# A gated mix of linear attention and SwiGLU: the third piece of wq and wk on ScalarE's DMA queue

## The chip, the cores and the metric

The kernel runs on one core of one Trainium2 chip. The metric is the device time of one execution, in microseconds (us), lower being better. A core has TensorE (PE, with weight loads listed apart as PEld), VectorE (DVE), ScalarE (ACT), GpSimd (POOL) and SyncE (SP). Every engine has an instruction stream of its own, and the streams meet only at semaphores. DMAs are issued by an engine's stream and carried out by 16 DMA engines that the queues share. In this kernel nearly all DMAs are issued by SP (queue q1 in the profile), and one by ACT (q10).

## The reference

One input x (2048 tokens of 512 values, bf16) goes through two blocks, and a gate mixes what they give. Multiplications are in bf16 and sums in fp32.

```python
def A(x, wqkv, wo):                     # 32 heads of 16
    q, k, v = split(x @ wqkv)
    phi = lambda t: where(t > 0, t + 1, exp(t)) + 1e-6
    pq, pk = phi(q), phi(k)
    kv, z = einsum("bhsd,bhse->bhde", pk, v), pk.sum(over tokens)
    o = (pq @ kv) / (pq . z + 1e-6)
    return o @ wo

def B(x, w1, w3, w2):                   # hidden size 1376
    return (silu(x @ w1) * (x @ w3)) @ w2

g = sigmoid((x * gate_w).sum(-1, keepdims=True))
out = g * A(x, wqkv, wo) + (1 - g) * B(x, w1, w3, w2)
```

## The kernel before, in words

**Stages.** The tokens are cut into 16 tiles of 128. In the first stage (0 to about 46 us of the span) each tile is projected onto k and q (`project`, the matmuls of line 183; the four contraction chunks of 128 are called `kc`), `phi` makes pk and pq of them with one ACT activation and two DVE instructions, and `g_step` (line 231) sums x-transposed times pk over all tokens into four PSUM banks. From these sums v's part follows later, so v itself is never computed. The second stage runs four blocks of 512 tokens: the SwiGLU matmuls (lines 303 and 309), and then the output matmuls of both blocks and the mix (lines 475, 492 and 498). Stores leave on SP's queue.

**The order.** The schedule is written by hand: the program's order of instructions on each engine is the order in which they run, and nothing is reordered. The waits between engines follow from what each instruction reads and writes, region by region of a tile.

**The start.** wq and wk lie side by side in one tile, `wqk`, of four contraction chunks; a "piece" is one chunk, 128 partitions by 1024 bf16 values (256 KB), loaded by one call of `load_wqk` (line 126). SP issues, in this order: x's first 256 tokens in natural layout (line 129), the four pieces, and then for each further tile a load of x that transposes it on the way (`load_xT`, line 123), with natural copies of x in between (line 141), and the weights of the later stages (lines 143 to 156). ACT's stream begins with an activation of one column, `act_pre` (line 130), whose result nobody reads and before which ACT loads its table. The next instruction of its stream is the issue of a small DMA of its own, `touch` (line 133), which reads the first 16 columns of pieces two to four into a tile that nobody reads. ACT's next work after that is line 380, a copy of a transposed part of x out of PSUM.

**PE at the start.** PE runs 13 matmuls on a constant (line 359), transposes the first 256 tokens of x by matmuls with an identity matrix (line 365), and then runs the k and q matmuls of the first two tiles interleaved by piece: four on the first piece, two transposes for the fourth chunk of x, four on the second piece, then k's two on the third and two on the fourth, and q's four on the third and fourth. The k projection of tile 2 follows, the first to use an x that SP's transposing loads brought.

```python
    for kc in range(2):
        for n, t in (("k", 0), ("q", 0), ("k", 1), ("q", 1)):
            first_mm(n, t, kc)
        if kc == 0:
            transpose_kc(3, bank[0])
            nc.vector.tensor_copy(out=xT[:, 3, 0 : 2 * P], in_=bank[0][:, 0 : 2 * P])
    for kc in range(2, KC):
        for t in range(2):
            first_mm("k", t, kc)
```

Of the kernel before, what the change touches and what calls it, by code (L numbers as in the profile page):

```python
# [8 lines left out]
ACT = mybir.ActivationFunctionType  # L9
# [3 lines left out]
BF16 = mybir.dt.bfloat16  # L13
# [3 lines left out]
def kernel(  # L17
# [17 lines left out]
    nc = tc.nc  # L35
    P = nc.NUM_PARTITIONS

    Bb, S, D = A_x.shape
# [23 lines left out]
    wqkv_r = A_wqkv.rearrange("(kc d) n -> d kc n", d=P)  # L62
# [3 lines left out]
    consts = ctx.enter_context(tc.tile_pool(name="consts", bufs=1))  # L66
# [5 lines left out]
    warm = nc.const_aps.tensor(1.0, [P, 256], BF16)  # L72
# [7 lines left out]
        out=bmask[:], in_=bmask[:], pattern=[[-Dh, HPC], [0, Dh]], compare_op=ALU.is_ge,  # L80
# [3 lines left out]
        out=bmask[:], in_=bmask[:], pattern=[[Dh, HPC], [0, Dh]], compare_op=ALU.is_ge,  # L84
# [23 lines left out]
    wqk = consts.tile([P, KC, 2 * D], BF16, name="wqk")  # L108
# [6 lines left out]
    w3 = consts.tile([P, KC, F0], BF16, name="w3")  # L115
    w2 = consts.tile([P, FC, D], BF16, name="w2")
    xT = consts.tile([P, KC, S], BF16, name="xT")
    act_pre = consts.tile([P, 1], BF16, name="act_pre")
    dq = nc.sync

    def load_xT(t):
        ts = slice(t * P, (t + 1) * P)
        dq.dma_start(out=xT[:, :, ts], in_=x2d[ts, :], transpose=True)

    def load_wqk(kc):
        dq.dma_start(out=wqk[:, kc, :], in_=wqkv_r[:, kc, 0 : 2 * D])

    x_first = x2d[0 : 2 * P, :].rearrange("(p j) d -> p j d", j=2)
    dq.dma_start(out=xN[:, 0:2, :], in_=x_first)  # L129
    nc.scalar.activation(out=act_pre[:], in_=warm[:, 0:1], func=ACT.Exp)  # L130

    touch = consts.tile([P, KC - 1, 16], BF16, name="touch")
    nc.scalar.dma_start(out=touch[:], in_=wqkv_r[:, 1:KC, 0:16])
    for kc in range(KC):
        load_wqk(kc)
    natural = {3: (2, 4), 5: (4, 8), 8: (8, 16)}
    for t in range(2, NT):
        load_xT(t)
# [3 lines left out]
    with nc.allow_non_contiguous_dma(reason="gate column"):  # L142
        dq.dma_start(
            out=wr[:, :, 2 * FR : NR], in_=gate_w.rearrange("(kc d o) -> d kc o", d=P, o=1)
# [3 lines left out]
    for w, w_r, cuts in ((w1, w1_r, (0, KC)), (w3, w3_r, (0, KC))):  # L148
# [8 lines left out]
        out=w2x[:].rearrange("p r d -> p (r d)"),  # L157
        in_=w2x_r[None].to_broadcast([TPB, RP, RG * D]),
# [442 lines left out]
```

## Time and profile before

| what | value |
|---|---|
| median of 3 runs | 178.73 us (178.44 to 178.74) |
| the profiled execution's own time | 177.74 us |
| its span, first to last instruction | 176.0 us |
| PE busy | 171.3 us, 97% |
| DVE, POOL, ACT busy | 110.5, 63.3, 59.1 us |
| first k matmul of PE | 4.41 us into the span |
| end of the first stage | about 46 us |

The profile is of one execution. Its times count from the first instruction of the span. A line of the timeline gives start, duration, engine, source line (L126 is line 126), operation, the tiles written and read, and in square brackets how long the engine had sat idle and what ended that; a "q" behind an engine's name (SPq, ACTq) marks an instruction of its sequencer, here a DMA issue. PE's matmuls are pipelined, so that the duration of one overlaps the next. The chain is the chain of work that ended last, followed back from the end. "Landing" is the time from the start of a DMA's issue to its completion semaphore.

### The profile page before, as it was taken

The numbers are of one execution on the slowest core, as the hardware profiler recorded it, in microseconds if no ns is written. First come the engines' busy times: TensorE is split into PE (matmuls) and PEld (weight loads), VectorE is DVE, ScalarE is ACT, GpSimd is POOL, SyncE is SP. The second block draws the span as 40 slices with busy tenths as digits, with TensorE's granted clock in tenths as the row PEclk, the third lists the DMA queues.
The fourth block names the chain that finished last, engine by engine and source line by source line (L and its number), as shares of the span: only waits on it lengthen the run. The fifth ranks groups of instructions, "written<-read, shape, count | busy, mean of one in ns | idle before, by whom it ended". The sixth has DMA issues, their size and how long they took to land.

```text
span 176.0 us, 2668 instructions
## 1 busy us (share of the span) xinstructions
PE 171.3 (97%) x952; PEld 82.4 (47%) x969; DVE 110.5 (63%) x207; ACT 59.1 (34%) x109; POOL 63.3 (36%) x106
## 2 busy tenths in 40 slices
PE   8999999999999999999999999999999999999993
PEld 5444444444456443444444466444444444444453
DVE  0399788888764899777343477853435775344363
ACT  4364544544753533322433101224226122422000
POOL 5087656656300668586300044540000662000000
DMA  5988969997205112323200013330000233000001
GB/s 172 277 197 207 164 123 237 403 352 231 78 4 56 22 30 41 78 63 91 58 0 0 0 34 84 84 89 0 0 4 0 60 89 89 4 0 0 30 30 60
DMA packets 29360, 15.58 MB, mean 88 GB/s; under 512 B 21156, under 2 KB 27556, under 8 KB 29348
## 3 DMA queue, kind: packets, MB, share of 16 engines
q1 hardware_dynamic: 28948, 15.41, 35.1%
q8 instruction: 7, 0.11, 0.3%
q10 hardware_dynamic: 400, 0.01, 0.1%
q14 instruction: 5, 0.04, 0.1%
HBM read 8.86 MB, written 2.10 MB: 62 GB/s over the span
## 4 chain that ended last, share of the span: by engine, by line
PE 95%; DMA 2%; issue 1%; SPq 0%; DVE 0%
PE bank L303 20%; PE bank L492 20%; PE bank L309 19%; PE bank L183 16%; PE bank L231 8%; PE bank L475 8%; PE bank L245 3%; DMA wqk<-in_A_wqkv_dram 2%; PE bank L278 2%; PE bank L447 0%; SPq L129 0%; PE bank L462 0%; DVE o L498 0%; PE bank L365 0%
## 5 line engine op out<-in xcount | busy, mean ns | idle before, releaser
L315 DVE TENSOR_TENSOR hT<-bank,sg 128x512 bf16<-128x512 f32 x40 | 27.3, 682 | 31.0 <-PE bank L309 28.9
L303 PE MATMUL bank<-xT,w 128*128 128x512 bf16 x158 | 40.8, 379 | 0.2
L309 PE MATMUL bank<-xT,w 128*128 128x512 bf16 x156 | 40.5, 379 | 0.2
L314 ACT ACTIVATE sg<-bank 128x512 bf16<-128x512 f32 x40 | 23.9, 597 | 45.9 <-PE bank L303 45.9
L492 PE MATMUL bank<-w,hT 128*128 128x512 bf16 (+2 forms) x176 | 37.0, 355 | 0.5 <-issue 0.3
L337 POOL TENSOR_TENSOR pqs<-pq,rden 128x512 bf16<-128x512 bf16 x16 | 16.9, 1057 | 54.3 <-issue 46.8
L183 PE MATMUL bank<-wqk,xT 128*128 128x512 bf16 x126 | 30.2, 379 | 0.1
L215 POOL TENSOR_TENSOR zacc<-zacc,pk 128x128 f32<-128x128 f32 x56 | 23.3, 447 | 10.4 <-DVE pk L201 10.4
L492 PEld LDWEIGHTS <-hT 128*128 128x128 bf16 x180 | 16.7, 98 | 18.4 <-issue 0.8
L309 PEld LDWEIGHTS <-w 128*128 128x128 bf16 x160 | 15.7, 98 | 18.9
L303 PEld LDWEIGHTS <-w 128*128 128x128 bf16 x160 | 15.5, 98 | 18.2 <-issue 0.2
L498 DVE SCALAR_TENSOR_TENSOR o<-bank,omg_all,aga 128x512 bf16<-128x512 f32 (+2 forms) x18 | 12.4, 692 | 14.5 <-PE bank L492 11.7
L183 PEld LDWEIGHTS <-xT 128*128 128x128 bf16 x128 | 12.5, 98 | 14.9 <-issue 0.3
L322 POOL TENSOR_TENSOR pr<-pq,zb 128x512 f32<-128x512 bf16 x16 | 18.4, 1155 | 0.1
L231 PE MATMUL bank<-pk,xN 128*128 128x512 bf16 x62 | 16.3, 379 | 0.2
L475 PE MATMUL bank<-M,pqT 128*128 128x512 bf16 x61 | 15.6, 379 | 0.1
L196 ACT ACTIVATE eq<-bank 128x512 bf16<-128x512 f32 x16 | 9.4, 597 | 16.0 <-PE bank L183 14.9
L201 DVE SCALAR_TENSOR_TENSOR pk<-bank,emk 128x512 bf16<-128x512 f32 x16 | 11.1, 692 | 1.6
L196 ACT ACTIVATE ek<-bank 128x512 bf16<-128x512 f32 x16 | 9.4, 597 | 6.5 <-PE bank L183 6.5
L201 DVE SCALAR_TENSOR_TENSOR pq<-bank,emq 128x512 bf16<-128x512 f32 x16 | 11.1, 692 | 0.5
L326 DVE TENSOR_REDUCE den<-pr 128x32 f32<-128x512 f32 x16 | 10.8, 676 | 0.0
L231 PEld LDWEIGHTS <-xN 128*128 128x128 bf16 x64 | 6.3, 98 | 7.5
(54 smaller groups left out, 95.6 us busy)
## 6 DMA issues: line engine op xcount, KB each, us to landing
w<-in_B_w_dram SPq DMA_DIRECT2D x3, 1280.0 KB, 10.3
out_dram<-o SPq DMA_DIRECT2D x15, 128.0 KB, 1.9
wqk<-in_A_wqkv_dram SPq DMA_DIRECT2D x4, 256.0 KB, 3.7
xN<-in_A_x_dram SPq DMA_DIRECT2D x1, 1024.0 KB
xN<-in_A_x_dram SPq DMA_DIRECT2D x2, 256.0 KB, 2.9
xN<-in_A_x_dram SPq DMA_DIRECT2D x1, 512.0 KB, 4.2
wv<-in_A_wqkv_dram SPq DMA_DIRECT2D x1, 512.0 KB, 11.2
wo<-in_A_wo_dram SPq DMA_DIRECT2D x1, 512.0 KB, 12.2
```

Source lines behind the costliest of these rows:

```text
L183: nc.tensor.matmul(ps[:], lhsT=xT[:, kc, t * P : (t + 1) * P], rhs=w[:, kc, :], start=(kc == 0), stop=(kc == KC - 1),)
L196: nc.scalar.activation(out=e[:], in_=ps[:], func=ACT.Exp)
L201: nc.vector.scalar_tensor_tensor(out=dst, in0=ps[:], scalar=0.0, in1=em[:], op0=ALU.max, op1=ALU.add)
L215: nc.gpsimd.tensor_tensor(out=(zaccb if t == NT - 1 else zacc)[:, cs], in0=zacc[:, cs], in1=pk[t][:, cs], op=ALU.add,)
L231: nc.tensor.matmul(bank[kc][:], lhsT=xN[:, t, kc * P : (kc + 1) * P], rhs=pk[t][:], start=(t == 0), stop=(t == NT - 1),)
L303: nc.tensor.matmul(g_ps[:], lhsT=w1[:, kc, fs], rhs=xT[:, kc, tok], start=(kc == 0), stop=(kc == KC - 1),)
L309: nc.tensor.matmul(u_ps[:], lhsT=w3[:, kc, fs], rhs=xT[:, kc, tok], start=(kc == 0), stop=(kc == KC - 1),)
L314: nc.scalar.activation(out=sg[:], in_=g_ps[:], func=ACT.Silu)
L315: nc.vector.tensor_tensor(out=hT[tb][:, fc, :], in0=u_ps[:], in1=sg[:], op=ALU.mult)
L322: nc.gpsimd.tensor_tensor(out=pr[t][:], in0=pq[:, t, :], in1=zb[:], op=ALU.mult)
L475: nc.tensor.matmul(ps[:], lhsT=pqT[:, c, ts], rhs=M2[:, c, :], start=(c == 0), stop=(c == KC - 1),)
L492: nc.tensor.matmul(ps[:, 0 : cs.stop - cs.start], lhsT=hT[tb][:, fc, tt * P : (tt + 1) * P], rhs=w2[:, fc, cs], start=(fc == 0 and not sta ...
```

## The change

The third piece (`kc` of 2) is issued on ACT's queue, and the other three stay on SP's in their order. ACT's first activation no longer writes a tile of its own but the first column of the third piece in `wqk`. The DMA that loads the third piece writes the same column, so it waits until that activation has finished. In ACT's stream it comes after `touch`. The tile `act_pre` goes.

```diff
@@ -115,24 +115,23 @@
-    act_pre = consts.tile([P, 1], BF16, name="act_pre")
     dq = nc.sync
...
-    def load_wqk(kc):
-        dq.dma_start(out=wqk[:, kc, :], in_=wqkv_r[:, kc, 0 : 2 * D])
+    def load_wqk(kc, queue):
+        queue.dma_start(out=wqk[:, kc, :], in_=wqkv_r[:, kc, 0 : 2 * D])
 
     x_first = x2d[0 : 2 * P, :].rearrange("(p j) d -> p j d", j=2)
     dq.dma_start(out=xN[:, 0:2, :], in_=x_first)
-    nc.scalar.activation(out=act_pre[:], in_=warm[:, 0:1], func=ACT.Exp)
+    nc.scalar.activation(out=wqk[:, 2, 0:1], in_=warm[:, 0:1], func=ACT.Exp)
 
     touch = consts.tile([P, KC - 1, 16], BF16, name="touch")
     nc.scalar.dma_start(out=touch[:], in_=wqkv_r[:, 1:KC, 0:16])
     for kc in range(KC):
-        load_wqk(kc)
+        load_wqk(kc, nc.scalar if kc in (2,) else dq)
```

## The prediction, made before the result was known

> **What bounds the kernel now.** I read the page's busy time and its chain first, then the chain from 3 to 10 us, then the start in order of time, then the transfers.
>
> ```profile
> PE 171.3 (97%) x952; PEld 82.4 (47%) x969; DVE 110.5 (63%) x207; ACT 59.1 (34%) x109; POOL 63.3 (36%) x106
> ...
> PE 95%; DMA 2%; issue 1%; SPq 0%; DVE 0%
> ```
>
> TensorE is busy for 97% of the span and makes 95% of the chain, so what shifts its stream near the start shifts the end by as much. The list of waits has none of PE on a DMA after 7 us that could take a shift back; its few idle spots later are waits on ACT and DVE, which follow PE, and lost records. The only DMA in the chain (2%) is one the change touches:
>
> ```profile
> 1.26 3.11 DMA wqk<-in_A_wqkv_dram
> 4.37 0.04 issue
> 4.41 1.02 PE bank L183 x4
> 5.43 0.11 PE bank L365 x2
> 5.54 3.60 PE bank L183 x16
> ```
>
> From 4.41 PE runs four matmuls on the first piece, two transposes, four on the second, two each on the third and fourth. A matmul of 512 columns follows the last after 0.216 us. The second piece's start at 5.38, the third's at 6.25, and the fourth's would at 6.68 but do at 6.83, after a weight load that sat idle:
>
> ```profile
> 6.83 0.96 PEld L183 LDWEIGHTS <-xT 128*128 128x128 bf16 x5 [0.27 <-issue]
> ```
>
> So the fourth piece costs PE 0.15 us and the others nothing. The issues at the start, SP's queue and ACT's:
>
> ```profile
> 0.81 0.39 SPq L129 DMA_DIRECT2D xN<-in_A_x_dram  x1
> 1.26 1.84 SPq L126 DMA_DIRECT2D wqk<-in_A_wqkv_dram  x4
> 3.15 1.30 SPq L123 DMA_TRANSPOSE xT<-in_A_x_dram  x1
> ```
>
> ```profile
> 0.80 1.28 ACT L130 ACT_TABLE_LOAD   x1 [0.80 <-PEq L585]
> 0.86 0.43 ACTq L133 DMA_DIRECT2D touch<-in_A_wqkv_dram  x1
> 2.10 0.20 ACT L130 ACTIVATE act_pre<-const-bfloat16-1.0 128x1 bf16<-128x1 bf16 x1
> ```
>
> The four pieces are issued at 1.26, 1.72, 2.20 and 2.67, 0.47 apart. The DMA view of a window with one issue in it gives each one's time to landing: 3.1, 3.4, 3.9 and 4.1 us. With the trace's own ends that is 4.37, 5.17, 6.06 and 6.78 (x landed at 3.60). They land 0.72 to 0.89 apart, so it is the transfer that paces them, not the issue. A piece is there 0.21 us (second) and 0.19 us (third) before use; that is all the slack.
>
> The queues between 2.9 and 3.2 us, q10 being ACT's and q1 SP's, with packets, MB and share of 16 engines:
>
> ```profile
> q10 hardware_dynamic: 359, 0.01, 67.3%
> q1 hardware_dynamic: 43, 0.06, 50.2%
> ```
>
> ACT's small DMA takes the engines when x is through, ahead of SP's first piece, and nearly alone: where both have work, one goes as a run and the other stands.
>
> **The change part by part.** *Removed:* a 128x1 tile; the activation stays, with the same size and its table load, and ends at 2.30. *SP's queue:* one issue fewer, so the fourth piece is issued at 2.20 and the transposed loads, natural x and weights behind it all 0.47 us sooner. PE waits for none of them: the first transposed load landed at 7.28 for a use at 8.12. Worth 0. If they were late instead, that 0.84 is the cover.
>
> *ACT's queue:* one issue of 0.43 us more. It waits for the activation: 2.30 plus 0.05 (from the releaser's end to an issue or matmul in these rows) is 2.35, so it ends near 2.79. Behind it stands ACT's copy of the transposed x (L380), which starts at 4.08 and waits 1.78 us for PE. 1.3 us of that is left over, so the cost is 0; without that cover it would be 0.43 on the way to the first q and k matmuls.
>
> *Where the third piece falls among the transfers* is the term that counts. From the end of its issue x took 0.72 us to its first packet (1.20 to 1.92, idle engines). ACT's touch took 1.6 us or more (1.29 to between 2.90 and 3.05), but x held the engines for that time. So the third piece stands at the engines between 2.79 + 0.72 = 3.5 and 2.79 + 1.6 = 4.4. I take 3.5, since the longer one has its reason in x. x's last bytes ran near 3.0 and it landed at 3.60; by that lag of some 0.5 us the first piece's bytes end near 3.85 and the second's near 4.65. At 3.5 the first piece is still running and the second stands queued.
>
> If ACT's queue gets its turn there, as touch did after x, the order of landings is first, third, second, fourth in the same four places, since the bytes are the same. The second then lands at 6.06 instead of 5.17. PE starts it at 6.06 + 0.04 = 6.10 instead of 5.38: +0.72. Four matmuls later, at 6.96, the third is long there; at 7.40 the fourth (6.78) is too, so the 0.15 us wait goes. Sum +0.72 - 0.15 = +0.57 us. Were the two queues to share packet by packet, the first would land later but the second still third, and the sum is the same.
>
> The Trainium skill has two rules on this, in "DMA: Bandwidth & Descriptors". "Issuing engines are not separate DMA queues" says that transfers from SP and ACT run on the same 16 engines, and a second issuer saves only issue time. The landings 0.72 to 0.89 us apart on issues 0.47 apart agree; by it the gain is 0 of the 0.47. "Queues, rings and completion order" says that each engine goes round the queues and empties a whole packet of descriptors before it switches. By that rule the third piece follows the first and the sum is +0.57; by order of age (the touch row, issued before the first piece, fits that as well) it is the +0.43 below.
>
> Ends: below, -0.15 (only the fourth piece's wait goes; PE cannot begin before 4.37, when its transposes end, so the first piece has 0.04 more at most). Above, +0.72 with 0.2 more for a switch of queues, the time that touch held the engines, less 0.15: about +0.8.
>
> **The sum** is against the profiled execution: 177.74 + 0.57 = 178.31, its span 176.0 + 0.57 = 176.6 and 1.74 around it. That execution lies 0.99 below the median of the three runs, so on the median: 178.73 + 0.57 = 179.30.
>
> **The rivals.**
> *Order of age.* The third piece's issue ends at 2.79, after the fourth's (2.20 to 2.63), and it goes last. It lands at 6.78, and PE, which takes it before the fourth, starts it at 6.83 instead of 6.25: +0.58 - 0.15 = +0.43, 179.16. For it: touch ran in order of age too. Against: it needs one line for both queues, and the page shows two.
>
> *Order kept.* If ACT's transfers do take 1.6 us from issue to engine, the third piece arrives at 4.4, during the second, and runs where it ran. Then 0 to -0.15: 178.6 to 178.73, no change. For it: the touch row is the only one on ACT's queue. A higher place of the same kind: should PE be on its slow clock longer in other executions (256 columns took 0.213 us before 3.6 us, 512 take 0.216 after 4.4), it would reach the second piece later and hide the late landing.
>
> *Faster.* Two queues leave fewer gaps at the engines: a 2 KB packet takes 84 ns, so a piece's 8 packets per engine need 0.67 us against 0.72 to 0.89. The fourth would land at 3.60 + 4 x 0.67 = 6.28 and nothing waits. In the profiled execution that is worth 0.15 + 0.04 at most, 0.1%. It decides only if the 0.99 us by which the shown runs lie above the profiled one is the same wait, and at least 0.17 us of it goes too; with half of it, 178.73 - 0.15 - 0.5 = 178.1. No row shows what those runs wait for.
>
> *The clock.* PE would stand still from 5.43 to 6.10. Should that bring back the slow rate for as long as it held at first (0.84 to about 4.1), it costs half of 3.3 us: 178.73 + 0.57 + 1.65 = 180.95. No row shows a stop of that length near the start.
>
> **How the numbers follow.** Third piece ahead of the second, +0.57: 0.42. Order of age, +0.43: 0.14. Order kept: 0.32. Faster: 0.07. Clock: 0.05. The forecast is the first, 179.3 us. A measurement of this kernel tells about 0.2% (0.36 us) from no change. So slower holds 0.42 + 0.14 + 0.05 = 0.61, less 0.03 for a second piece that lands some 0.2 us sooner than I take: 0.58. Within 0.2%: 0.35. Faster: 0.07. The range takes in the kept order with the 0.15 gain and a spread of 0.2 below (178.4), and reaches above the forecast by 0.3, to the upper end of +0.8 and a little spread (179.6). It leaves out the clock and most of faster, some 0.15 with the noise. The forecast's own range is 179.1 to 179.6.
>
> **What would show it.** ACT's issue of the third piece at 2.35, SP's transposes from 2.67. Landings: second near 6.06, third near 5.17, fourth near 6.8. A PE wait for the second piece of 0.6 to 0.7 us ending near 6.1 and none at the fourth; PE's first matmul at 4.41 as before. Wrong if the second still lands by 5.4: then the order was kept. A wait before the third piece to about 6.8 is the order of age.

## The result and the profile after

The change makes the kernel slower: the median goes from 178.39 us to 179.12 us over 22 runs each, a ratio of 1.0045 with a 95% interval of 1.0034 to 1.0056. That is 0.6 to 1.0 us. The forecast was +0.57.

The page of the changed kernel's profiled execution (178.61 us, span 176.8), busy times and chain:

```profile
PE 173.1 (98%) x969; PEld 82.5 (47%) x969; DVE 110.9 (63%) x207; ACT 59.1 (33%) x109; POOL 63.2 (36%) x106
...
PE 96%; DMA 2%; DVE 0%; issue 0%
```

TensorE is still the bound, and no other engine has over 0.4 us more work (the 1.8 us more of PE go with 17 matmul records more than in the profile before, and with a slower start, below). The issues at the start, ACT's and SP's (line numbers are one lower than before):

```profile
0.87 0.44 ACTq L132 DMA_DIRECT2D touch<-in_A_wqkv_dram  x1
2.10 0.20 ACT L129 ACTIVATE wqk<-const-bfloat16-1.0 128x1 bf16<-128x1 bf16 x1
2.33 0.36 ACTq L125 DMA_DIRECT2D wqk<-in_A_wqkv_dram  x1
```

```profile
0.81 0.39 SPq L128 DMA_DIRECT2D xN<-in_A_x_dram  x1
1.25 1.37 SPq L125 DMA_DIRECT2D wqk<-in_A_wqkv_dram  x3
2.67 1.30 SPq L122 DMA_TRANSPOSE xT<-in_A_x_dram  x1
```

The change did what it says: the third piece is issued at 2.33, 0.03 us after the activation, and SP's transposed loads start 0.47 us sooner. What landed when, by the trace's own ends, is the core of the matter. "First G" is PE's first matmul on pk (L231 before), and "rest" the span from there to its end:

| profile | first | second | third | fourth | first G | rest |
|---|---|---|---|---|---|---|
| before | 4.37 | 5.17 | 6.06 | 6.78 | 8.98 | 167.06 |
| changed, 1st | 4.53 | 5.19 | 7.08 | 6.68 | 9.71 | 167.07 |
| changed, 2nd (after_again) | 4.46 | 5.13 | 6.99 | 6.81 | 9.61 | 167.06 |
| changed, 3rd (after_third) | 4.35 | 6.58 | 7.63 | 7.50 | 10.26 | 167.06 |

The rest of the kernel is 167.06 to 167.15 us in all 14 profiles of this study, whatever came ahead. So all that the change costs within the span is lost before the first G, as the forecast had it, and nothing is given back.

A smaller part lies outside the span. Every run has its time and its span on record (spans to 0.1 us). The time is longer than the span by 1.85 us on the mean in the changed kernel (1.80 to 1.92 in single runs), and by 1.71 in the kernel before (1.65 to 1.78). So 0.14 of the 0.73 us is spent where no view looks; on what, is not shown.

Where it is lost depends on the execution. The chain of the first profile of the changed kernel, from 3 us on:

```profile
0.81 2.99 DMA xN<-in_A_x_dram
3.79 0.05 issue
3.84 0.82 PE bank L364 x6
4.66 1.54 PE bank L182 x4
6.21 0.11 PE bank L364 x2
6.32 3.55 PE bank L182 x16
```

There is no piece in it. x landed 0.19 us later than in the profile before, and the four matmuls on the first piece took 1.54 us, not 1.02: PE's slow clock lasted to about 6 us. PE came to the third piece at 7.02 and waited 0.10 us for it. So this pair of profiles, 0.73 us apart at the first G, shows hardly any of what the change costs; that the difference fits is chance. (The kernel before without touch, with all pieces on SP's queue and the slow clock too, has its first G at 9.70.) The third profile, whose time (179.17 us) is nearest to the median, shows the cost:

```profile
1.72 4.86 DMA wqk<-in_A_wqkv_dram
6.58 0.04 issue
6.62 1.02 PE bank L182 x4
7.64 0.03 issue
7.67 2.75 PE bank L182 x12
```

PE waits for the second piece until 6.62, and after it for the third, whose first matmul starts at 7.67. The row of PE's wait in the timeline:

```profile
6.62 1.64 PE L182 MATMUL bank<-wqk,xT 128*128 128x512 bf16 x6 [0.83 <-DMA wqk<-in_A_wqkv_dram]
```

How the transfers ran is seen in a window from 4.8 to 5.6 us. Before:

```profile
DMA packets 159, 0.30 MB, mean 371 GB/s; under 512 B 14, under 2 KB 14, under 8 KB 159
## 3 DMA queue, kind: packets, MB, share of 16 engines
q1 hardware_dynamic: 159, 0.30, 96.7%
```

and in the first profile of the changed kernel:

```profile
DMA packets 136, 0.28 MB, mean 348 GB/s; under 512 B 0, under 2 KB 0, under 8 KB 136
## 3 DMA queue, kind: packets, MB, share of 16 engines
q10 hardware_dynamic: 67, 0.14, 50.5%
q1 hardware_dynamic: 69, 0.14, 46.9%
```

A piece is 128 packets of 2 KB, and ends on each engine with one packet of 4 bytes. Before, 14 such ends fall into these 0.8 us. After, the two queues move nearly the same number of packets and no engine ends any piece. So in this profile third and fourth run in turn and end together. They land 0.40, 0.18 and 0.12 us apart in the three profiles, against 0.72 before. The second profile is less clean. There the fourth ended on 12 of the 16 engines within the same window, and had landed on 15 by 6.18; it landed at 6.81 because of one engine. The third, too, had its last packet on one engine half a microsecond after those on the others (6.54 against 6.06).

### The profile page after: what moved, and what is told of

It is laid out like the page before. It is cut to its first block, busy times and chain, and to the rows that moved or that the text cites. A ratio compares the mean times of both kernels' runs of the same rounds, so it can differ in the third digit from the quotient of the medians.

```text
span 176.8 us, 2685 instructions
## 1 busy us (share of the span) xinstructions
PE 173.1 (98%) x969; PEld 82.5 (47%) x969; DVE 110.9 (63%) x207; ACT 59.1 (33%) x109; POOL 63.2 (36%) x106
## 4 chain that ended last, share of the span: by engine, by line
PE 96%; DMA 2%; DVE 0%; issue 0%
PE bank L491 20%; PE bank L302 20%; PE bank L308 20%; PE bank L182 16%; PE bank L230 8%; PE bank L474 8%; PE bank L244 3%; DMA xN<-in_A_x_dram 2%; PE bank L277 2%; PE bank L364 1%; PE bank L446 0%; PE bank L461 0%; DVE o L497 0%
## 5 line engine op out<-in xcount | busy, mean ns | idle before, releaser
L302 PE MATMUL bank<-xT,w 128*128 128x512 bf16 x160 | 41.1, 379 | 0.0
L308 PE MATMUL bank<-xT,w 128*128 128x512 bf16 x160 | 41.1, 379 | 0.0
L491 PE MATMUL bank<-w,hT 128*128 128x512 bf16 (+2 forms) x180 | 37.5, 355 | 0.0
L182 PE MATMUL bank<-wqk,xT 128*128 128x512 bf16 x128 | 31.0, 384 | 0.0
L474 PE MATMUL bank<-M,pqT 128*128 128x512 bf16 x64 | 16.1, 379 | 0.0
```

Of the source, the lines that this page charges most:

```text
L182: nc.tensor.matmul(ps[:], lhsT=xT[:, kc, t * P : (t + 1) * P], rhs=w[:, kc, :], start=(kc == 0), stop=(kc == KC - 1),)
L302: nc.tensor.matmul(g_ps[:], lhsT=w1[:, kc, fs], rhs=xT[:, kc, tok], start=(kc == 0), stop=(kc == KC - 1),)
L308: nc.tensor.matmul(u_ps[:], lhsT=w3[:, kc, fs], rhs=xT[:, kc, tok], start=(kc == 0), stop=(kc == KC - 1),)
L474: nc.tensor.matmul(ps[:], lhsT=pqT[:, c, ts], rhs=M2[:, c, :], start=(c == 0), stop=(c == KC - 1),)
L491: nc.tensor.matmul(ps[:, 0 : cs.stop - cs.start], lhsT=hT[tb][:, fc, tt * P : (tt + 1) * P], rhs=w2[:, fc, cs], start=(fc == 0 and not sta ...
```

## The experiments

Each run shares its comparison with runs of the kernel before on the same chip. The times to landing and first packets are from each run's one profile.

**A second profile, the hold alone, PE's order turned, the fourth piece moved.** The first theories were that the third piece is late (L), that PE's clock is what differs (C), and that the hold costs the time (H).

*after_again* is the changed kernel unaltered.

> The changed kernel once more, for a second profile of it. Theory L (late piece): the third piece stands at the engines only some 1.8 us after its issue ends, shares them packet by packet with the fourth, and lands last, at 6.9 to 7.2 us; PE waits for it, so the ratio is 1.003 to 1.006, and in an execution whose PE is on its fast clock by 4.4 us the wait ahead of the third piece's first matmul is 0.6 to 0.9 us. Theory C (clock): the changed kernel is slower since PE's fast clock comes later in it (5.9 us in the profile after against about 4.1 before); then matmuls 0.43 us apart on the first piece are seen here too, and the third piece's landing costs 0.1 us or nothing.

1.0046 (1.0031 to 1.0062). The third landed at 6.99, last. PE's clock was slow to about 5.7 us here too, and the wait at the third piece only 0.11. As far as this profile goes, C was not ruled out.

*hold_on_sp* has the activation write into the third piece, and all four pieces on SP's queue:

```diff
-        load_wqk(kc, nc.scalar if kc in (2,) else dq)
+        load_wqk(kc, dq)
```

> The hold alone: the activation writes into the third piece, all four pieces stay on SP's queue. SP's third issue moves from 2.20 to 2.35 us and all behind it by 0.15. Theory L: the transfer paces the pieces, so the third still lands near 6.06 and the fourth near 6.8; ratio 0.999 to 1.001. Theory H (the hold is what costs): the third piece lands later by the hold and PE waits; ratio 1.003 to 1.005.

1.0005 (0.9987 to 1.0024). The pieces landed at 4.32, 4.97, 5.63 and 6.40, in order. The hold, 0.13 us on SP's queue, costs nothing that could be measured.

*after_pe_swap* lets PE take the fourth piece ahead of the third:

```diff
...
-    for kc in range(2, KC):
+    for kc in (3, 2):
         for t in range(2):
             first_mm("k", t, kc)
...
-    for kc in range(2, KC):
+    for kc in (3, 2):
         first_mm("q", 0, kc)
-    for kc in range(2, KC):
+    for kc in (3, 2):
         first_mm("q", 1, kc)
```

The accumulations of these matmuls end on the third piece instead of the fourth.

> The changed kernel, but PE takes the fourth piece ahead of the third for the first two tiles; no DMA differs from the changed kernel. Theory L: the fourth (landed 6.68) is used from about 6.7, the third (7.08) from about 7.15, four or so matmuls of 0.216 us lie between what is there and what is late, and most of the loss goes: ratio 1.000 to 1.002. Theory C or one in which SP's earlier transposed loads cost the time: ratio stays 1.0035 to 1.0055.

1.0042 (1.0021 to 1.0062): nothing came back, and L in that form fell. The ratio is the one that C gave. In this profile, however, the fast clock was there by 5.1 us: the second piece landed at 6.50 and PE waited for it, and the fourth (7.48) was as late as the third (7.66).

*fourth_on_act* moves the fourth piece instead of the third (the hold with it):

```diff
-    nc.scalar.activation(out=wqk[:, 2, 0:1], in_=warm[:, 0:1], func=ACT.Exp)
+    nc.scalar.activation(out=wqk[:, 3, 0:1], in_=warm[:, 0:1], func=ACT.Exp)
...
-        load_wqk(kc, nc.scalar if kc in (2,) else dq)
+        load_wqk(kc, nc.scalar if kc in (3,) else dq)
```

> The fourth piece instead of the third on ACT's queue, held by the activation writing into it; the third on SP's. Theory L: the fourth comes to the engines near 4.5 us, shares them with the third, and lands last near 7.1, the third near 6.7; PE starts the third at about 6.72 instead of 6.25 and the fourth at 7.12 instead of 6.83: +0.3 us, ratio 1.001 to 1.003. A theory by which ACT's queue takes its turn right after the first piece: the fourth lands second, third and second piece a place later, ratio 1.003 to 1.004.

1.0040 (1.0027 to 1.0053), more than expected. The second landed at 5.05, so ACT's queue did not take its turn after the first piece. The third, although it stayed on SP's queue, landed at 7.13, the fourth at 7.50. PE's clock was fast by 4.4 us, and the wait stands alone in PE's timeline:

```profile
5.41 1.03 PE L182 MATMUL bank<-wqk,xT 128*128 128x512 bf16 x4
7.17 0.59 PE L182 MATMUL bank<-wqk,xT 128*128 128x512 bf16 x2 [0.74 <-DMA wqk<-in_A_wqkv_dram]
```

Here the loss is there with a fast clock, so C does not explain it. Sharing may not be all of it either. The third had landed on 13 of the 16 engines by 6.14, and three reads of 2 KB took 0.70, 0.85 and 1.23 us (between 4.15 and 4.28, ahead of ACT's first packet), against the usual 84 ns. From this came theory S: a piece on ACT's queue makes the piece beside it late as well, whichever of the two is moved; both end when the last byte is there.

**What the joint landing costs without ACT's queue.** *pair_on_sp* is the kernel before with third and fourth loaded by one DMA on SP's queue:

```diff
-    for kc in range(KC):
+    for kc in range(2):
         load_wqk(kc)
+    dq.dma_start(out=wqk[:, 2:4, :], in_=wqkv_r[:, 2:4, 0 : 2 * D])
```

> The kernel before, with the third and the fourth piece loaded by one DMA of 512 KB on SP's queue, so that both are there only when the last byte is; ACT's queue carries no piece. Theory S (sharing): what the change costs is first of all that the third piece, moved packet by packet beside the fourth, lands with it at the end of all four instead of a place ahead. Then this kernel shows that part alone: both land near 6.8, PE starts the third at about 6.83 instead of 6.25 and does not wait for the fourth, +0.43 us, ratio 1.001 to 1.0035. If the late landing of both costs nothing by itself: 0.999 to 1.001.

1.0034 (1.0019 to 1.0048), 0.6 us. Both landed at 6.62, earlier than the fourth did before, and PE waited for them in front of the third:

```profile
5.76 0.86 PE bank L184 x4
6.63 0.03 issue
6.66 2.75 PE bank L184 x12
```

```profile
6.66 1.39 PEld L184 LDWEIGHTS <-xT 128*128 128x128 bf16 x7 [0.31 <-issue]
```

This is the experiment that carries the explanation. It has no second queue, no hold and, in its profile, no later last byte (SP's transposed loads start 0.47 us sooner here too, on which see the next run). What it takes away is the third piece's place ahead of the fourth. Its time outside the span is that of the kernel before (1.71). Within the span its runs are 0.56 us longer on the mean than those of the kernel before, and those of the changed kernel 0.56 and 0.68 (in *after_third* and *after_again*). The interval is wide, 0.34 to 0.86 us, and the expected 0.43 lies in it. Its profile shows less: PE waited 0.19 us (a matmul was due at 6.47), and the first G came 0.27 later than before. But that execution, 178.10 us, was the fastest of 12, and no profile shows where a middling one loses its time.

**When ACT's transfer comes to the engines.** In the four profiles so far with a held piece on ACT's queue, its first 2 KB packet ran at 4.58 to 4.68 us, 1.9 to 2.0 after the issue's end. *xt_late* holds SP's first transposed load:

```diff
+    nc.gpsimd.memset(xT[:, 0, 2 * P : 2 * P + 1], 0.0)
     x_first = x2d[0 : 2 * P, :].rearrange("(p j) d -> p j d", j=2)
```

> The changed kernel, with SP's first transposed load held by a write of GpSimd into one column of its destination, so that it is issued near 3.5 us instead of 2.67; the third piece is issued as in the changed kernel (2.33 to 2.69). In four profiles with a piece on ACT's queue its first 2 KB packet ran at 4.58 to 4.68 us, 0.61 to 0.71 after the end of SP's first transposed load's issue (3.95 to 3.97), the lag that x has after its own (0.64 to 0.73). Theory D (one writer of descriptors for both queues, and ACT's request waits behind SP's transposed load): the first packet comes at 3.3 to 3.6. Theory Q (ACT's queue takes some 1.9 us from the end of an issue whatever SP does): it stays at 4.5 to 4.7. Time: by D the third piece shares with the first and second, second lands late, ratio 1.001 to 1.005; by Q the transposed load no longer runs beside it, ratio 1.002 to 1.004.

The transposed load was issued at 3.39, and the first packet of the third piece still came late, at 4.82. So theory D fell. The ratio was 1.0043 (1.0023 to 1.0062), just over what Q gave; third and fourth landed at 7.15 and 6.97. SP's transposed loads start later here than in the kernel before (3.39 against 3.15), so their earlier start isn't the cause in the changed kernel either.

*no_hold* gives the activation its own tile again and leaves the third piece on ACT's queue:

```diff
-    nc.scalar.activation(out=wqk[:, 2, 0:1], in_=warm[:, 0:1], func=ACT.Exp)
+    nc.scalar.activation(out=act_pre[:], in_=warm[:, 0:1], func=ACT.Exp)
```

> The third piece on ACT's queue, not held: the activation writes a tile of its own, the issue follows touch at about 1.31 to 1.75 us. Theory Q: its first packet at 3.5 to 3.7, so it shares the engines with the first and second pieces, which land 0.3 to 0.8 us late; ratio 1.002 to 1.006. Theory D: its descriptors are written between two of SP's pieces, first packet at 2.9 to 3.3, the first piece lands near 5 us; ratio 1.003 to 1.008. Theory H (the hold is what costs): ratio 0.998 to 1.001.

First packet at 3.61, 1.76 after the issue's end: as Q had it. 1.0026 (1.0008 to 1.0044). But the third did not share with the second, as Q had expected. ACT's queue ran alone between the first and the second piece, as this window from 4.0 to 4.25 us shows, in which SP's queue has no packet:

```profile
q10 hardware_dynamic: 46, 0.09, 94.7%
```

The third had landed on 15 of the 16 engines by 5.07, and the second, behind it, by 5.75. One engine brought them only at 6.44 and 6.64 (one read on ACT's queue took 1.01 us, at 3.85), and the fourth landed at 7.18. So this run has the order that was forecast for the changed kernel, and each piece went as a run. It is slower than the kernel before all the same, though 0.14 of the 0.46 us lies outside the span (1.85 against 1.71).

*after_no_touch* and *before_no_touch* leave touch out of the changed kernel and of the kernel before:

```diff
-    touch = consts.tile([P, KC - 1, 16], BF16, name="touch")
-    nc.scalar.dma_start(out=touch[:], in_=wqkv_r[:, 1:KC, 0:16])
```

> The changed kernel without ACT's small DMA (touch) ahead of the third piece. Theories D and Q: the third piece's first packet stays at 4.5 to 4.7, it shares with the fourth, ratio 1.003 to 1.006. Theory T (the 384 rows of touch stand before it in ACT's queue and delay it): first packet near 3.4, shared with the first and second pieces, ratio 1.000 to 1.006.

> The kernel before without touch: touch held the engines from 2.93 to 3.2 us, ahead of the first piece. All theories: the pieces land up to 0.2 us sooner unless their first reads are slower without it; PE waits for the fourth piece alone (0.15 us) and cannot begin before x lands, so ratio 0.998 to 1.002; the counterpart of the run without touch on the changed kernel.

After without touch: 1.0066 (1.0044 to 1.0088), just above what the theories gave. The first packet came at 3.95, between their figures and 1.24 after the issue's end, so by this profile touch does stand in the way for some 0.5 to 0.9 us, though half of the piece's packets ran only after 5.5. The second was joined and landed at 6.82. Before without touch: 1.0007 (0.9989 to 1.0026), pieces at 4.31, 5.55, 6.59 and 7.34. Whether touch is worth anything to the changed kernel stays open, since the intervals with and without it overlap (1.0034 to 1.0056, 1.0044 to 1.0088).

*x_on_act* puts x's first load on ACT's queue, where nothing stands before it:

```diff
-    dq.dma_start(out=xN[:, 0:2, :], in_=x_first)
+    nc.scalar.dma_start(out=xN[:, 0:2, :], in_=x_first)
```

> The kernel before, with x's first load issued on ACT's queue (ahead of the activation and of touch) instead of SP's; all four pieces on SP's. It measures how long ACT's queue takes from an issue to the first packet when nothing stands before it. Theory Q (the queue itself is slow): first packet of x 1.6 to 2.1 us after its issue ends, near 2.9 to 3.3, so x lands near 4.3 and everything waits for it; ratio 1.003 to 1.007. Rival (ACT's transfers were late only since SP's stood before them): first packet 0.65 to 0.75 after, near 1.9, x shares the engines with the first piece and lands near 4.0 to 4.4; ratio 1.001 to 1.005.

Both theories missed. The queues of this run from 1.6 to 2.25 us, and from 2.25 to 2.4:

```profile
q1 hardware_dynamic: 23, 0.05, 44.7%
```

```profile
q10 hardware_dynamic: 10, 0.02, 45.5%
q1 hardware_dynamic: 8, 0.02, 37.9%
```

Both issues ran from 0.80 to 1.20. SP's first packet came at 1.84, ACT's at 2.30: 0.64 and 1.09 after the end. So ACT's queue came 0.45 us later than SP's with nothing ahead of it, against 1.24 us from the end of the issue to the packet in the changed kernel without touch, and 1.7 to 2.1 behind touch. Whether the queue itself is slower, or of two requests made at once one is served after the other, this run can't tell. The time was 1.0048 (1.0012 to 1.0085), which both theories allowed.

**Both late pieces on ACT's queue.** *two_on_act* is xt_late with third and fourth on ACT's queue, one behind the other:

```diff
-        load_wqk(kc, nc.scalar if kc in (2,) else dq)
+        load_wqk(kc, nc.scalar if kc in (2, 3) else dq)
```

> The third and the fourth piece both on ACT's queue, one behind the other, held as in the changed kernel; SP's first transposed load issued near 3.4 us, as in the run with the late transposed load, so that little runs beside them. Theory S: nothing shares the engines with the third piece, so it lands a place ahead of the fourth, third 5.8 to 6.2, fourth 6.5 to 6.9; ratio 0.999 to 1.0015. Theory Q alone (ACT's queue is late by 1.9 us and that is the cost): the engines stand idle until 4.6 to 4.8, third at 6.3 to 6.6, fourth at 7.0 to 7.4; ratio 1.002 to 1.004.

1.0025 (1.0007 to 1.0042), which tells nothing apart. 0.32 of these 0.45 us lie outside the span (2.03 against 1.71). In its profile the second landed at 6.80, beside the third (7.32), and the fourth at 8.04. So there was sharing after all, with the second, and the run did not test what it was made for.

**A third profile.** *after_third* is the changed kernel unaltered.

> The changed kernel a third time, for one more profile. Theory S: third and fourth piece land within 0.5 us of each other at the end of all four, whatever the second does; if the second lands at 5.0 to 5.2 the third's first matmul follows the third's landing by 0.04, and if the second is late (over 6 us, as in the run with PE's order turned) PE waits for that one. PE's first matmul of L230 comes 0.6 to 1.2 us later than the 8.98 of the kernel before, and span less that start is 167.0 to 167.2 as in the others.

1.0035 (1.0018 to 1.0052). Third and fourth ended 0.12 us apart, and the second was late; the chain is shown above. The first G came 1.28 us after the 8.98 of before, a little beyond what was expected. None of the kernels of this study was faster than the kernel before.

## Why the prediction was right, and where not

*The sign, the place and the size.* Slower, by a PE wait in the stretch of the four pieces that shifts all that follows one to one: shown by the rest of 167.06 to 167.15 us in every profile. The 0.57 us was too small: 0.73 by the medians, 0.80 by the ratio. That the time forecast, 179.30, is only 0.18 above the measured 179.12 is in part luck: the three runs that it started from lay 0.34 above the median of the 22.

*The time around the span.* The forecast kept it at 1.74 us. It rose by 0.14, and it goes with the number of DMAs that ACT's queue carries. The mean is 1.72 us with none (before without touch), 1.71 and 1.69 with one (the kernel before; the changed kernel without touch), 1.84 to 1.88 with two (x on ACT's queue; the changed kernel and its variants with one piece there), and 2.03 with three. So some 0.6 us of the cost falls into the stretch that the forecast was about.

*What SP's and ACT's moved issues cost.* Nothing, as forecast: ACT's copy of x waited 1.97 us for PE behind the new issue (1.78 before), and the first transposed load landed at 7.30 for a use at 8.84.

*The fourth piece's 0.15 us.* Gone, as forecast: PE does not stop for the fourth where the third came later.

*Where the third piece falls.* Here two steps failed for the changed kernel. "I take 3.5, since the longer one has its reason in x": the first packet came at 4.39 to 4.82 in the six profiles with one held piece on ACT's queue behind touch. The touch row, the other end, was the right one, and x was not its reason: x's bytes were long through by then, and with x itself on ACT's queue, and nothing ahead of it, ACT's first packet still came 0.45 us later than SP's of the same moment. The other step was "one goes as a run and the other stands". The touch packets had gone so, and so does the third piece where it is not held, but in the changed kernel it went in turn with the fourth. When queues go in turn and when as a run, these traces do not settle. The sentence that the sum would be the same if they shared packet by packet was meant for a third piece that joins the second; this one joins the fourth, and lands with it.

*The order of landings.* Forecast: first, third, second, fourth, with the second at 6.06 and PE's wait until 6.10. No profile of the changed kernel shows this order. The third profile has the wait for the second, half a microsecond later (6.58 and 6.62). But the third had not gone ahead of it: the second had landed on 15 of the 16 engines by 5.40, the third landed last, and PE then waited for it too, which the forecast had long there. In the first two profiles the second was on time, by which the prediction itself called its order wrong ("if the second still lands by 5.4"). The third was last, which is the place that the order of age gave it (+0.43, landing at 6.78; it was 7.08 and 6.99), for another reason. So the time came out near the forecast by another path, and the term was not one delay but one of two, by execution. In six profiles of a single held piece on ACT's queue with touch, counting the one with PE's order turned and the one with the late transposed load, the second was late in two. Runs on SP's queue alone had it at 4.97 to 5.17, and without touch at 5.55.

*Why the second is late in some.* In those two profiles one read of 2 KB took 0.99 us (at 3.50) and 1.35 us (at 3.86), against the usual 84 ns, before ACT's first packet of the piece. If that engine still has rows of the second piece when ACT's come, they go in turn. Long reads (0.62 at 4.50) are in the profile before too, and with SP alone a 0.80 us one left the second at 5.55. This is argued from these rows, and no run shows it.

*The order kept.* Its arrival (4.4) was right and its consequence wrong: the third came during the end of the second, but ran beside the fourth, not ahead of it.

*The clock.* A stop did not bring the slow rate back: after its wait until 7.17 the kernel with the fourth piece on ACT's queue ran matmuls 0.216 apart. The other way round C keeps a part that is open: the slow rate lasted past 5.6 us in five of the nine profiles with a piece on ACT's queue and in one of the five without, too few to say whether the change brings it.

*The rules of the Trainium skill.* "DMA: Bandwidth & Descriptors", "Issuing engines are not separate DMA queues", says that the queues' transfers interleave and a second issuer saves only issue time: the 67 and 69 packets of the two queues in the first profile agree. "Queues, rings and completion order" says that an engine empties a whole packet of descriptors of one queue before it turns to the next. If that packet is a piece's eight rows on an engine, as the forecast had it, that profile disagrees: one of the two pieces would have ended on each engine between 4.8 and 5.6, and none did. The run without the hold agrees: ACT's queue moved 46 packets between 4.0 and 4.25 us, and SP's none.

*What stays open.* How the 0.7 to 0.8 us is made up over many executions. Each run keeps one profile, in which PE's clock, x's landing, the long reads and the second piece differ, and no profile of the kernel before lies at its own median. What is spent outside the span is open too.

## What to carry to other kernels

Loads that are used one after another belong on one queue in that order. On two queues they ran on the same engines, in turn or one ahead of the other as they happened to arrive, and in no run here was that faster. Where the transfers are paced by the engines (0.72 to 0.89 us a piece here) and not by the issue (0.47), a second queue had nothing to give. And where a few tenths of a microsecond at the start decide, one profile of each side is not a comparison; look at more than one, and at what all of them have in common.

## What was not expected of the hardware

ACT's queue took longer to its first packet than SP's: 1.09 against 0.64 us after the end of an issue made at the same moment, and 1.7 to 2.1 behind a DMA of 384 rows of 32 bytes. And the second and the third DMA on ACT's queue went with 0.14 and 0.18 us more outside the span.

PE's rate at the start differs between executions: matmuls of 512 columns were 0.427 us apart until 5.7 to 6.2 us in six of the 14 profiles, and 0.216 apart from 5.1 at the latest in the others, while the mean granted clock reads 0.998 to 1.000 in all. One of the six has all pieces on SP's queue; the timeline of the kernel before without touch, on the first piece:

```profile
4.37 1.89 PE L181 MATMUL bank<-wqk,xT 128*128 128x512 bf16 x4
```

These four took 1.02 us in the profile before. The Trainium skill's "TensorE: Matmul & The Clock Gate", Part 1, says that the slow rate lasts for about 3.4 us of activity, and that the window by which it is judged runs free of the kernel's start; what is seen here, 3.3 to 5.4 us after PE's first matmul at 0.84, starts at that figure and spreads as a free-running window would have it. Where PE is slow that long, it hides a late piece: 0.10 us of waiting in the first profile of the changed kernel, 0.74 and more with a fast PE.
